# A fused Nystrom attention and mixture-of-experts kernel: halved first loads, landmark trees on VectorE, a W2 half placed later, one ending tile loaded as it lies, and last copies split over two engines

## The chip, the cores and the metric

The kernel runs on one core of a Trainium2 chip. The metric is the device time of one execution in microseconds (us). A run of the profiler gives one execution with every instruction's start and duration; other executions are only timed. PE is TensorE (PEld its weight loads), DVE is VectorE, ACT is ScalarE, POOL is GpSimd and SP is SyncE; a "q" behind a name (SPq, DVEq) means the sequencer of that engine, which waits, branches and issues transfers.

## The reference

The inputs are q, k and v, each 8 batches x 8 heads x 576 positions x 64 (float32), two gate matrices 512x8, and for 8 experts W1 (512x1024) and W2 (1024x512). Cut to what matters:

```python
q_lm = q.reshape(B, H, 32, 18, D).mean(axis=3)        # landmarks: means of 18 rows
k_lm = k.reshape(B, H, 32, 18, D).mean(axis=3)
A, Bm, C = sm(q, k_lm), sm(q_lm, k_lm), sm(q_lm, k)   # softmax of scaled products
Z = Bm.T / (norm1(Bm) * norminf(Bm) + 1e-6)
for _ in range(6):
    Z = 2 * Z - Z @ Bm @ Z
x = (A @ Z @ C @ v)                                   # then laid out as 4608 tokens x 512
e_idx = argmax(x @ w_gate)                            # one expert for each token
out[tok] = softmax(x @ w_gate)[e_idx] * sigmoid((x @ w_output_gate)[e_idx]) * (relu(x @ w1[e]) @ w2[e])
```

## The kernel before, in words

The attention works on 16 groups of one batch and four heads. A group's q and k lie in the upper part of the big expert weight tile `W` (three experts' worth of it, called `tail`, holds attention data until it is free for weights). `load` (L211) issues q, k and v of a group on SP; q and k have two pairs of places, so a load waits until the group two before it has been turned. The first two groups are loaded at the very start, in the order q, k, v, q, k, v. A load of `zeros` into the sorted token buffer `x_sorted` (L163) stands ahead of them in the source, and after the first q and k in SP's order.

`landmark_sums` (L224) adds the 18 rows of each landmark as a tree of five adds on POOL; for group 0 alone DVE makes the sum with one reduction (L948). `landmarks` (L236) scales a sum on ACT and writes it twice side by side. `transposes` (L243) turns a q or k on PE into two PSUM tiles of four blocks and one of two, of which the last block is the landmark; ACT copies each PSUM tile out (L257), and there are two such PSUM tiles in turn (`ps_t`). Then come the score products (L265, L280), the softmaxes, the iteration for Z (L359 to L379, small matmuls with a DVE step between), and the products that give a token's 512 values and its gate logits (L422). `routing` picks the expert of each token on DVE and POOL scatters token rows to `x_sorted` by expert (L530).

The expert part works on tiles of 128 tokens of one expert. Tiles come in stages: 8 and 10 tiles of the fullest two experts, then 8 "free" tiles, all while the attention still runs, and an ending whose number of tiles depends on the data. An ending is one arm of a switch (L967): each engine reads the number of the arm from memory, and jumps to its own code for it. In the profiled run the ending has 12 tiles. For a tile of the first stages `fetch` (L670) loads x as it lies and `turn_x` (L694) turns it with four PE transposes and a DVE copy; an ending tile's x is instead loaded by a transposing transfer (L680). `up` makes h (L720, or L709 in the first two stages), `turn_h` (L725) turns it with eight PE transposes and one DVE copy (L730), `down` (L732) multiplies by W2 in eight matmuls (L737), which can be issued as two halves of four, scales the result on DVE (L743), and POOL scatters the rows to the output (L745). Weights are loaded and cast by POOL's transfers, four pieces an expert (L142 for W1, L145 for W2).

The order of the work is written out by hand. Each kind of work is a generator, and the string `ORDER` (L20) lists which generator makes its next step: L loading, G landmark sums, M landmark scaling, T transposes, C and A the two softmaxes, N the iteration, O outputs, R routing, E weight loads, X expert tiles. A generator that needs an event not yet recorded skips its turn. What comes out is one fixed order of instructions on each engine; each engine works through its own in order and waits at semaphores.

Of the kernel before, what the change touches and what calls it, by code (L numbers as in the profile page):

```python
# [8 lines left out]
F32 = mybir.dt.float32  # L9
# [10 lines left out]
ORDER = (  # L20
    "TTTGTTLTMCTGCTTACGCMCATTCTLMATCCTLAAAAGTCALCMTTCTCNGANLMCNATCGTLALCAACTGMCLTTANTLAMNCCTLGCANCNNLTCAN"
    "AANMGTCCTNNLTATAOLGAMCCNLGATOAACCTMAGNOCANTLTACTMNTANCLMNONNCACNLACNGOTTCGTMCANOALONTTATLOCCNOATNCGA"
    "AMNOCTRRCTCNARLRMNRTTTRLARCLNTNGCMNRRLGRRCRARAAACTCNCLTRTNLRNTAGOTLMATNRTEENRCRCONRCRNAGCNONTAMAACCG"
    "AEOTXTATNONLXCAALNCMGATTACCOTCAEAEXXOMXCOOLXTNMATXGAOLLRTRTNXERGLAXCXXMTXCNTRGCACRMTECCTAATNRARXMNCC"
    "XNXXNARRLTCENTAXCEXNXLTACTXLGTXARAALNLRGRETXXCNXMTNGCNAAXXONRXETXCNXNXAOLXANAOTNRAXNACOMNCGXTONCEXML"
    "TNALCRTXAGOCCXLXOTXXAMCXCAXGRETOCAOXXRCOTNNTTTXXERNXERCMNXXRRXXANREETXEXCNXRXARCRNXRRAXEMXEXREAETXXT"
    "CTXNXTRNRCTXRNXXXCLXAXEXCCEXXXXCRNCOXCEAAOAXXACXXXXXNEAXXAXXEXNOEXXEONXXNXXEOANRXXXXRXXNXXXRENXNXANE"
    "XXXXAXNXXXNAXXOXOOXOXXXOXRRRRRXRXXXXRXXRXXXXRRXXXRRRXXXXXXXXXRRXXXXXXRXXXXXXXRRXXXXXXXXXXXX"
)
# [3 lines left out]
def kernel(  # L33
# [11 lines left out]
    nc = tc.nc  # L45
# [177 lines left out]

    def landmark_sums(k, nm):  # L224
        G = groups[k]
        t = G[nm]
        s = sa.tile([128, hg, D], F32, tag="lms", bufs=1, name="lms")
        s1 = sa.tile([128, 1, D], F32, tag="lm1", bufs=2, name="lm1")
        nc.gpsimd.tensor_tensor(s, t[:, :hg, :], t[:, hg:, :], op=OP.add)  # L229
        nc.gpsimd.tensor_tensor(s[:, 0:4, :], s[:, 0:4, :], s[:, 4:8, :], op=OP.add)  # L230
        nc.gpsimd.tensor_tensor(s[:, 0:2, :], s[:, 0:2, :], s[:, 2:4, :], op=OP.add)
        nc.gpsimd.tensor_tensor(s[:, 0:1, :], s[:, 0:1, :], s[:, 1:2, :], op=OP.add)
        nc.gpsimd.tensor_tensor(s1, s[:, 0:1, :], s[:, 8:9, :], op=OP.add)
        G["s" + nm] = s1
# [8 lines left out]
    def transposes(k):  # L243

        G = groups[k]
        for nm in ("q", "k"):
            tv = G[nm].rearrange("p (gp par) d -> p gp (par d)", par=2)
            lm = G["l" + nm].rearrange("p a d -> p (a d)")
            at = turned_places[(2 * k + (nm == "k")) % 3]
            tT = tail[:, at:at + TW].rearrange("p (c x) -> p c x", x=128)  # L250
            G[nm + "T"] = tT
            for c0 in range(0, hg + 1, 4):
                n = min(4, hg + 1 - c0)
                p = ps_t.tile([128, 4, 128], F32, tag="tp", name="tp")
                for i in range(n):
                    nc.tensor.transpose(p[:, i, :], in_=tv[:, c0 + i] if c0 + i < hg else lm, identity=I128)  # L256
                nc.scalar.copy(tT[:, c0:c0 + n, :], p[:, :n, :])  # L257
                yield
# [191 lines left out]
    def routing(pair):  # L450
# [216 lines left out]
    last = len(SLOTS)  # L667
    xs_bf = xs.bitcast(BF16)

    def fetch(t):  # L670
# [53 lines left out]

    def turn_h(t):  # L725
        pt = ps_t.tile([128, FCH, 128], BF16, tag="tp", name="pt")
        for fc in range(FCH):
            nc.tensor.transpose(pt[:, fc, :], in_=t["h"][:, fc], identity=Ibf)  # L728
        t["hT"] = mp.tile([128, FCH, 128], BF16, tag="h", bufs=3, name="hT")
        nc.vector.tensor_copy(t["hT"], pt)  # L730

    def down(t, part=None):  # L732
        if part != 1:
# [6 lines left out]
        if part == 0:  # L740
            return
        y = mp.tile([128, HD], F32, tag="y", bufs=4, name="y")
        nc.vector.tensor_scalar(out=y, in0=t["py"], scalar1=t["coef"],  # L743
                                scalar2=None, op0=OP.mult)
        i = nc.gpsimd.indirect_dma_start(  # L745
            out=out, out_offset=bass.IndirectOffsetOnAxis(ap=t["id"], axis=0),
# [15 lines left out]
    def summing():  # L762
        for k in range(1, NGRP):
            for nm in "qk":
                yield from need("loaded " + nm, k)
                yield from need("marked " + nm, k - 1)
                landmark_sums(k, nm)
# [12 lines left out]
    def turning():  # L780
        for k in range(NGRP):
            for i, _ in enumerate(transposes(k)):
                if i % 3 == 2:
                    mark("turned " + "qk"[i // 3], k)
                yield
                nxt = 6 * k + i + 1
                if nxt < 6 * NGRP and nxt % 3 == 0:
                    to, half = nxt // 6, nxt % 6 // 3
                    yield from need("marked " + "qk"[half], to)
                    if to + half >= 2:  # L790
# [83 lines left out]
    def working():  # L874
        for stage, n in enumerate(SLOTS):
# [12 lines left out]
            for j, t in enumerate(tiles):  # L888
# [9 lines left out]
                if stage >= len(RANKS):  # L898
                    turn_h(t)
                    yield  # L900
# [45 lines left out]
    for nm in "qk":  # L946
        s1 = sa.tile([128, 1, D], F32, tag="lm1", bufs=2, name="lm1")
        nc.vector.tensor_reduce(s1[:, 0, :], groups[0][nm].rearrange("p g d -> p d g"), axis=AX.X, op=OP.add)  # L948
        groups[0]["s" + nm] = s1
        landmarks(0, nm)  # L950
        mark("marked " + nm, 0)
    for c in ORDER:
# [14 lines left out]
    for arm in tc.Switch(tables["which"], len(ENDINGS), hint="ending"):  # L967
# [40 lines left out]
```

## Time and profile before

| | |
|---|---|
| median of 3 runs | 377.08 us (375.72 to 377.74) |
| the profiled execution's own time | 376.81 us |
| its span, first to last instruction | 375.2 us |
| mean granted TensorE clock | 0.985 |
| PE busy | 323.5 us (86%) |
| DVE, ACT, POOL busy | 221.2, 175.0, 215.5 us |
| moved by the transfers | 66.76 MB, mean 178 GB/s |
| attention and first stages | 0 to about 282 us |
| free tiles alone | about 282 to 318 us |
| ending, 12 tiles | 318.4 us to the end |

A row of the timeline gives start, duration, engine, line, operation, result and inputs, shapes and count, and in brackets how long the engine was idle before it and what ended that. Rows of several like instructions are merged. A row of the waits gives the sum, the number and the longest. A row of the stretches gives, for each engine, busy time and instructions, then the granted PE clock, the share of the 16 transfer engines that was busy and the GB/s. The profiled execution is close to the median of the timed ones, so its stretches can be read as those of an ordinary run.

### The profile page before, as it was taken

The numbers are of one execution on the slowest core, as the hardware profiler recorded it, in microseconds if no ns is written. First come the engines' busy times: TensorE is split into PE (matmuls) and PEld (weight loads), VectorE is DVE, ScalarE is ACT, GpSimd is POOL, SyncE is SP. The second block draws the span as 40 slices with busy tenths as digits, with TensorE's granted clock in tenths as the row PEclk, the third lists the DMA queues.
The fourth block names the chain that finished last, engine by engine and source line by source line (L and its number), as shares of the span: only waits on it lengthen the run. The fifth ranks groups of instructions, "written<-read, shape, count | busy, mean of one in ns | idle before, by whom it ended". The sixth has DMA issues, their size and how long they took to land. (4 is left out here: it accounts for less than half of the span.)

```text
span 375.2 us, 11946 instructions
## 1 busy us (share of the span) xinstructions
PE 323.5 (86%) x4532; PEld 208.1 (55%) x4532; DVE 221.2 (59%) x584; ACT 175.0 (47%) x413; POOL 215.5 (57%) x319
## 2 busy tenths in 40 slices
PE   2888879888888877999998899999979997899992
PEld 1555456565655645676666477666645553455551
DVE  6277677477977384777658672665635674223322
ACT  2676475766737553554555354543234331232320
POOL 3788855644887487278888465784420585122322
PEclk9999899999989998999999999999999999999999
DMA  8866555245637997895587799999992357354221
GB/s 254 268 192 207 176 190 168 71 145 190 184 145 139 293 261 156 216 236 202 116 243 190 146 243 255 228 229 247 228 259 89 117 180 172 64 91 121 73 86 50
DMA packets 46743, 66.76 MB, mean 178 GB/s; under 512 B 16208, under 2 KB 35024, under 8 KB 46672
## 3 DMA queue, kind: packets, MB, share of 16 engines
q0 software_dynamic: 17568, 31.24, 37.4%
q1 hardware_dynamic: 29104, 34.63, 31.9%
q8 instruction: 39, 0.64, 0.7%
q14 instruction: 32, 0.26, 0.3%
HBM read 65.35 MB, written 16.23 MB: 217 GB/s over the span
## 5 line engine op out<-in xcount | busy, mean ns | idle before, releaser
L745 POOL DMA_INDIRECT out_dram<-y,ic x38 | 39.1, 1030 | 88.1 <-DVE y L743 69.9
L737 PE MATMUL py<-W,hT 128*128 (+1 forms) x304 | 73.9, 382 | 6.9 <-DMA W<-in_moe_w_dram 4.0
L743 DVE TENSOR_SCALAR y<-py,ic 128x512 f32<-128x512 f32 x38 | 28.4, 749 | 60.2 <-PE py L737 59.9
L257 ACT COPY W<-tp 128x512 f32<-128x512 f32 (+1 forms) x96 | 47.9, 515 | 31.9 <-PE tp L256 31.6
L256 PE MATMUL tp<-ident,W 128*128 128x128 f32 x288 | 51.2, 298 | 13.3 <-ACT W L257 7.8
L229 POOL TENSOR_TENSOR lms<-W 128x576 f32<-128x576 f32 x30 | 43.0, 1435 | 31.6 <-DMA W<-in_q_dram 30.6
L737 PEld LDWEIGHTS <-hT 128*128 128x128 bf16 x304 | 29.1, 99 | 39.1 <-issue 6.6
L723 ACT ACTIVATE h<-ph 128x512 bf16<-128x512 f32 x40 | 23.9, 597 | 56.0 <-PE ph L720 51.2
L256 PEld LDWEIGHTS tp<-ident,W 128*128 128x128 f32 x288 | 34.5, 148 | 24.5 <-ACT W L257 12.3
L530 POOL DMA_INDIRECT x_sorted<-row,r_slot x36 | 36.7, 1020 | 13.5 <-POOL row L528 8.8
L709 PE MATMUL ph<-xT,W 128*128 128x128 bf16 x576 | 37.7, 219 | 1.5 <-DMA W<-in_moe_w_dram 0.7
L422 PE MATMUL po<-vbd,AT 64*128 64x160 f32 (+1 forms) x320 | 32.8, 324 | 4.4 <-DVE L L428 3.4
L709 PEld LDWEIGHTS <-W 128*128 128x128 bf16 x576 | 33.2, 98 | 4.8 <-issue 2.6
L428 DVE TENSOR_REDUCE L<-po 128x16 f32<-128x128 f32 (+1 forms) x40 | 11.6, 290 | 40.2 <-ACT row L426 40.2
L712 ACT ACTIVATE hT<-ph 128x512 bf16<-128x512 f32 x36 | 21.4, 597 | 27.8 <-PE ph L709 27.6
L426 ACT CAST row<-po 128x512 bf16<-128x512 f32 (+1 forms) x40 | 23.4, 585 | 21.1 <-PE po L422 17.6
L265 PE MATMUL S<-W 64*32 64x288 f32 x512 | 26.1, 466 | 5.7 <-ACT BC L290 4.1
L359 PE MATMUL pw<-WV 32*32 32x96 f32 (+1 forms) x768 | 25.6, 249 | 5.6 <-DVE WV L379 3.4
L422 PEld LDWEIGHTS po<-vbd,AT 64*128 64x128 f32 (+1 forms) x320 | 22.5, 178 | 11.8 <-DVE L L428 5.7
L230 POOL TENSOR_TENSOR lms<-lms 128x256 f32<-128x256 f32 x30 | 24.9, 830 | 2.4
L359 PEld LDWEIGHTS pw<-WV 32*32 32x32 f32 x768 | 15.5, 107 | 16.0 <-DVE WV L379 7.4
L720 PE MATMUL ph<-W,x 128*128 x96 | 22.7, 379 | 1.7 <-DMA out_dram<-y,ic 1.3
(166 smaller groups left out, 530.0 us busy)
## 6 DMA issues: line engine op xcount, KB each, us to landing
W<-in_moe_w_dram POOLq DMA_DIRECT2D x32, 512.0 KB, 11.2
W<-in_q_dram SPq DMA_DIRECT2D x16, 576.0 KB, 6.6
W<-in_k_dram SPq DMA_DIRECT2D x16, 576.0 KB, 6.7
W<-in_v_dram SPq DMA_DIRECT2D x16, 576.0 KB, 5.2
x<-x_sorted SPq DMA_DIRECT2D x26, 128.0 KB, 6.4
x_sorted<-zeros SPq DMA_DIRECT2D x9, 136.0 KB, 1.9
ic<-x_sorted SPq DMA_DIRECT2D x38, 1.0 KB, 5.5
out_dram<-y,ic POOLq DMA_INDIRECT x38, 2.9
```

The lines of the kernel that those rows point to most:

```text
L229: nc.gpsimd.tensor_tensor(s, t[:, :hg, :], t[:, hg:, :], op=OP.add)
L230: nc.gpsimd.tensor_tensor(s[:, 0:4, :], s[:, 0:4, :], s[:, 4:8, :], op=OP.add)
L256: nc.tensor.transpose(p[:, i, :], in_=tv[:, c0 + i] if c0 + i < hg else lm, identity=I128)
L257: nc.scalar.copy(tT[:, c0:c0 + n, :], p[:, :n, :])
L265: nc.tensor.matmul(p[hs, par, :hg * 32], lhsT=lhs[pr, hg, hs], rhs=cols(rhs[pr, :hg, hs]))
L359: nc.tensor.matmul(p[hs, gi, lo:32 + D], lhsT=cur[hs, gi, :32], rhs=cur[hs, gi, lo:])
L422: nc.tensor.matmul(po[ps, hp, gi * 2 * VC:(gi + 1) * 2 * VC], lhsT=ATs[gi][hs, 128 * c:128 * c + n], rhs=vbd[hs, gi].rearrange("p a b -> p ...
L530: i = nc.gpsimd.indirect_dma_start(out=xs, out_offset=bass.IndirectOffsetOnAxis(ap=slot[:, c:c + 1], axis=0), in_=rows[c], in_offset=None)
L709: nc.tensor.matmul(ph[:, 128 * i:128 * i + 128], lhsT=columns(t, dc * F + (half * FCH // 2 + i) * 128, 128), rhs=t["xT"][:, dc, :], start= ...
L737: nc.tensor.matmul(t["py"], lhsT=t["hT"][:, fc, :], rhs=columns(t, DCH * F + fc * HD, HD), start=(fc == 0), stop=(fc == FCH - 1))
L743: nc.vector.tensor_scalar(out=y, in0=t["py"], scalar1=t["coef"], scalar2=None, op0=OP.mult)
L745: i = nc.gpsimd.indirect_dma_start(out=out, out_offset=bass.IndirectOffsetOnAxis(ap=t["id"], axis=0), in_=y, in_offset=None, bounds_check= ...
```

## The change

Five things change.

1. Group 0's q and k are each loaded by two transfers of half the columns, one issued by SP and one by ACT. In SP's order the first v then comes ahead of the zeros.
2. Group 0's landmark sums are made by the same tree of five adds as the other groups', on DVE instead of POOL. The scaling of k's landmark, which stood ahead of the first three PSUM copies on ACT, is now the first step of the generator M, and follows them (a letter M is put into `ORDER`). In `transposes` the landmark is looked up only when its block comes.
3. Two X steps move later in `ORDER`: the second half of the first tile's W2 product and the turn of a following x. On PE, four L737 matmuls and four L697 transposes now stand behind four L256 transposes, ten L359 and L364 matmuls, two more L256 and three L298 transposes. On DVE the y scaling and the xT copy move behind the start of an iteration and a routing step. On POOL the output scatter of that tile moves behind one tree of landmark sums.
4. The first tile of every ending (`LAID = 1`) is loaded as it lies, and turned by `turn_x` inside the arm: four PE transposes and a DVE copy ahead of its first L720.
5. The last free tile's and the last ending tile's hT copies, and the last ending tile's y scaling, are split: DVE makes the first half, ACT the second.

A temporary of the routing also shares its buffer with an earlier one.

```diff
 ORDER = (
-    "TTTGTTLTMCTGC...
+    "TTTMGTTLTMCTGC...
...
-    "...OLLRTRTNXERGLAXCXXMTXCNTRGCACRMTECC...
+    "...OLLRTRTNXERGLAXCXMTCNTRGCXXACRMTECC...
...
-            nc.sync.dma_start(out=t, in_=src.rearrange("h (m g) d -> (h m) g d", g=g))
+            lies = src.rearrange("h (m g) d -> (h m) g d", g=g)
+            if k == 0:
+                nc.sync.dma_start(out=t[:, :hg], in_=lies[:, :hg])
+                nc.scalar.dma_start(out=t[:, hg:], in_=lies[:, hg:])
+            else:
+                nc.sync.dma_start(out=t, in_=lies)
...
-    def landmark_sums(k, nm):
+    def landmark_sums(k, nm, eng):
...
-        nc.gpsimd.tensor_tensor(s, t[:, :hg, :], t[:, hg:, :], op=OP.add)
+        eng.tensor_tensor(s, t[:, :hg, :], t[:, hg:, :], op=OP.add)
...
-        zz = rt.tile([128, CPP, E], F32, tag="r_zz", name="r_zz")
+        zz = rt.tile([128, CPP, E], F32, tag="r_w8", name="r_zz")
...
+    LAID = 1
...
-        if s < last:
+        if s < last or i < LAID:
             ld = nc.sync.dma_start(out=x, in_=xs_bf[bass.ds(row, 128), :HD])
             t["x"] = x
...
-    def turn_h(t):
+    def turn_h(t, split=False):
...
+        if split:
+            nc.vector.tensor_copy(t["hT"][:, :FCH // 2], pt[:, :FCH // 2])
+            nc.scalar.copy(t["hT"][:, FCH // 2:], pt[:, FCH // 2:])
+            return
         nc.vector.tensor_copy(t["hT"], pt)
...
-    def down(t, part=None):
+    def down(t, part=None, split=False):
...
+        n = HD // 2 if split else HD
-        nc.vector.tensor_scalar(out=y, in0=t["py"], scalar1=t["coef"],
+        nc.vector.tensor_scalar(out=y[:, :n], in0=t["py"][:, :n], scalar1=t["coef"],
                                 scalar2=None, op0=OP.mult)
+        if split:
+            nc.scalar.activation(out=y[:, n:], in_=t["py"][:, n:], func=COPY, scale=t["coef"])
...
     def marking():
+        landmarks(0, "k")
+        mark("marked k", 0)
+        yield
...
-                    turn_h(t)
+                    turn_h(t, split=stage == last - 1 and j + 1 == n)
...
     for nm in "qk":
-        s1 = sa.tile([128, 1, D], F32, tag="lm1", bufs=2, name="lm1")
-        nc.vector.tensor_reduce(s1[:, 0, :], groups[0][nm].rearrange("p g d -> p d g"), axis=AX.X, op=OP.add)
-        groups[0]["s" + nm] = s1
-        landmarks(0, nm)
-        mark("marked " + nm, 0)
+        landmark_sums(0, nm, nc.vector)
+    landmarks(0, "q")
+    mark("marked q", 0)
...
             if j == 0:
+                turn_x(t)
                 both(t)
-            turn_h(t)
+            turn_h(t, split=j + 1 == len(run))
...
-            down(t)
+            down(t, split=j + 1 == len(run))
```

More of the change, by code (lines that the diff above doesn't have):

```diff
@@ L20 @@
 ORDER = (
[L21 to L28, printed above, removed]
+    "TTTMGTTLTMCTGCTTACGCMCATTCTLMATCCTLAAAAGTCALCMTTCTCNGANLMCNATCGTLALCAACTGMCLTTANTLAMNCCTLGCANCNNLTCA"
+    "NAANMGTCCTNNLTATAOLGAMCCNLGATOAACCTMAGNOCANTLTACTMNTANCLMNONNCACNLACNGOTTCGTMCANOALONTTATLOCCNOATNCG"
+    "AAMNOCTRRCTCNARLRMNRTTTRLARCLNTNGCMNRRLGRRCRARAAACTCNCLTRTNLRNTAGOTLMATNRTEENRCRCONRCRNAGCNONTAMAACC"
+    "GAEOTXTATNONLXCAALNCMGATTACCOTCAEAEXXOMXCOOLXTNMATXGAOLLRTRTNXERGLAXCXMTCNTRGCXXACRMTECCTAATNRARXMNC"
+    "CXNXXNARRLTCENTAXCEXNXLTACTXLGTXARAALNLRGRETXXCNXMTNGCNAAXXONRXETXCNXNXAOLXANAOTNRAXNACOMNCGXTONCEXM"
+    "LTNALCRTXAGOCCXLXOTXXAMCXCAXGRETOCAOXXRCOTNNTTTXXERNXERCMNXXRRXXANREETXEXCNXRXARCRNXRRAXEMXEXREAETXX"
+    "TCTXNXTRNRCTXRNXXXCLXAXEXCCEXXXXCRNCOXCEAAOAXXACXXXXXNEAXXAXXEXNOEXXEONXXNXXEOANRXXXXRXXNXXXRENXNXAN"
+    "EXXXXAXNXXXNAXXOXOOXOXXXOXRRRRRXRXXXXRXXRXXXXRRXXXRRRXXXXXXXXXRRXXXXXXRXXXXXXXRRXXXXXXXXXXXX"
 )
@@ L228, in landmark_sums @@
         s1 = sa.tile([128, 1, D], F32, tag="lm1", bufs=2, name="lm1")
[L229 to L233, printed above, removed]
+        eng.tensor_tensor(s, t[:, :hg, :], t[:, hg:, :], op=OP.add)
+        eng.tensor_tensor(s[:, 0:4, :], s[:, 0:4, :], s[:, 4:8, :], op=OP.add)
+        eng.tensor_tensor(s[:, 0:2, :], s[:, 0:2, :], s[:, 2:4, :], op=OP.add)
+        eng.tensor_tensor(s[:, 0:1, :], s[:, 0:1, :], s[:, 1:2, :], op=OP.add)
+        eng.tensor_tensor(s1, s[:, 0:1, :], s[:, 8:9, :], op=OP.add)
         G["s" + nm] = s1
@@ L253, in transposes @@
                 n = min(4, hg + 1 - c0)
+                if c0 + n > hg:
+                    lm = G["l" + nm].rearrange("p a d -> p (a d)")
                 p = ps_t.tile([128, 4, 128], F32, tag="tp", name="tp")
@@ L766, in summing @@
                 yield from need("marked " + nm, k - 1)
-                landmark_sums(k, nm)
+                landmark_sums(k, nm, nc.gpsimd)
                 mark("summed " + nm, k)
@@ L786, in turning @@
                 nxt = 6 * k + i + 1
+                to, half = nxt // 6, nxt % 6 // 3
+                if nxt < 6 * NGRP and nxt % 3 == 2:
+                    yield from need("marked " + "qk"[half], to)
                 if nxt < 6 * NGRP and nxt % 3 == 0:
-                    to, half = nxt // 6, nxt % 6 // 3
-                    yield from need("marked " + "qk"[half], to)
+                    yield from need("loaded " + "qk"[half], to)
                     if to + half >= 2:
```

1 line of the change is left out of this document (removed).

## The prediction

> **What bounds the kernel now.** I read the page's busy times first, then the waits of PE, then the timelines of the three places that the change touches.
>
> ```profile
> PE 323.5 (86%) x4532; PEld 208.1 (55%) x4532; DVE 221.2 (59%) x584; ACT 175.0 (47%) x413; POOL 215.5 (57%) x319
> ```
>
> ```profile
> PE tp L256 <- ACT W L257: 7.8, 11, 2.9
> PE tp L256 <- DMA W<-in_q_dram: 4.8, 1, 4.8
> ...
> PE py L737 <- DMA W<-in_moe_w_dram: 4.0, 1, 4.0
> ...
> PE ph L709 <- DMA W<-in_moe_w_dram: 0.7, 1, 0.7
> ```
>
> PE is busy for 86% of the span and works through one fixed order, so it sets the end: time that PE gains at a place is kept unless something else is late behind it. Its large waits are few: 4.8 us for the first q, one of 2.9 us for an ACT copy, one of 4.0 us for a W2 piece. The sum below counts, for each place, how much earlier or later PE reaches the work behind it.
>
> **The start (parts 1 and 2).**
>
> ```profile
> 4.71 4.11 DVE L948 TENSOR_REDUCE lm<-W 128x64 f32<-128x1152 f32 x2 [1.65 <-DMA W<-in_q_dram]
> 23.99 0.76 DVE L333 TENSOR_TENSOR At<-At,a_su 128x576 f32<-128x576 f32 x1
> 29.86 0.23 DVE L350 TENSOR_TENSOR BC<-BC,mB 128x64 f32<-128x64 f32 x1
> ...
> 8.86 0.31 ACT L239 ACTIVATE lm<-lm 128x128 f32<-128x128 f32 x1 [1.68 <-DVE lm L948]
> 9.07 1.05 ACT L257 COPY W<-tp 128x512 f32<-128x512 f32 x2
> 14.19 0.31 ACT L239 ACTIVATE lm<-lm 128x128 f32<-128x128 f32 x1 [1.13 <-POOL lm L233]
> ...
> 9.69 0.47 PE L256 MATMUL tp<-ident,W 128*128 128x128 f32 x1 [2.93 <-ACT W L257]
> 15.47 0.27 PE L256 MATMUL tp<-ident,lm 128*128 128x128 f32 x1
> ...
> 10.62 1.41 POOL L229 TENSOR_TENSOR lms<-W 128x576 f32<-128x576 f32 x1 [6.33 <-DMA W<-in_q_dram]
> ```
>
> ```profile
> 3.00:4.00 1.00, 0.00 (x0) 0.00 (x0) 0.06 (x1) 0.00 (x0) 0.88 (x8) 1.00 1.00 406
> 9.00:10.00 1.00, 0.31 (x2) 0.29 (x2) 0.00 (x0) 1.00 (x3) 0.00 (x0) 1.00 1.00 401
> ```
>
> PE has eight blocks turned by 6.8, but the copies that free their PSUM wait behind k's landmark (8.86), which waits for the second of two reductions of 2.05 us. After the change only q's landmark stands ahead. Its tree, by the 576-wide row (0.76) and the 64-wide one (0.23), is 0.76 + about 0.43 + 0.29 + 0.23 + 0.23 = 1.94 us (the two middle ones interpolated by width), so q's sum is there at 6.65 and the copies start near 6.9 instead of 9.07: 2.2 us.
>
> PE cannot keep that. Group 1's q landmark is written on ACT at 14.19 to 14.50, behind a POOL tree that begins when q of group 1 lands (10.62). PE would want it at 15.47 - 2.2 = 13.3 and gets it at about 14.55. **Gain 0.9 us.** I let that landing stay: the transfer engines are already full from 3 to 10 us, and halving a transfer adds no bytes. The two extra issues on ACT and the swap of v and zeros on SP I cost at nothing: ACT's first need is at 6.7, and the same bytes stand ahead of group 1's q. That the halves bring the first q in no sooner costs nothing for the same reason: even 0.5 us later, PE would still be ahead of that landmark. Queued behind the wait at 14.55 are the score products of group 0 and group 1's k, and through them SP's later loads, which move with PE. Bounds of the gain: 0 (PE cools in the wait that is left, below) and 2.2 (the landing moves too).
>
> **The W2 half (part 3).**
>
> ```profile
> 137.87 1.04 PE L737 MATMUL py<-W,hT 128*128 128x512 bf16 x4
> 142.94 1.87 PE L737 MATMUL py<-W,hT 128*128 128x512 bf16 x4 [4.03 <-DMA W<-in_moe_w_dram]
> 144.60 1.06 PE L256 MATMUL tp<-ident,W 128*128 128x128 f32 x4
> 145.46 0.56 PE L697 MATMUL pt<-ident_bf,x 128*128 128x128 bf16 x4
> ...
> 147.55 0.72 PE L265 MATMUL S<-W 64*32 64x288 f32 x16
> ...
> 140.45 0.76 DVE L284 TENSOR_REDUCE nm<-S 128x1 f32<-128x576 f32 x1
> 146.18 0.75 ACT L288 ACTIVATE eC<-S,nm 128x576 f32<-128x576 f32 x1
> ```
>
> ```profile
> 40.00:44.00 4.00, 2.58 (x56) 1.81 (x47) 2.39 (x8) 1.76 (x5) 3.61 (x6) 0.93 0.67 248
> 44.00:48.00 4.00, 4.00 (x89) 2.25 (x87) 3.21 (x6) 2.01 (x6) 3.61 (x6) 0.65 0.00 1
> ...
> 143.00:144.00 1.00, 1.00 (x3) 0.34 (x3) 0.00 (x0) 0.00 (x0) 0.80 (x3) 0.50 1.22 195
> ```
>
> The work that now fills the wait takes 147.55 - 144.60 = 2.95 us, less 0.49 for L697, which moves along with the half: 2.46 of 4.03 us. Its last part needs eC: nm is ready at 141.2, eC 0.75 later at about 142.0, the three transposes end near 142.5, still ahead of the weights at 142.9. So the half starts when it did, relative to the weights, and what followed it is already done: 2.46 us. The weights themselves come as much earlier as POOL issues them, and POOL works behind loads that wait for PE, so the 0.9 us of the start stays on top. Besides, four matmuls took 1.87 us here against 1.04 before the wait: the granted clock fell to 0.50. If the clock stays up, another 0.83 us: 3.3 us. The longest wait left is some 1.5 us (for eC), less than half of the old one. I take the warm end, **gain 3.3 us**, and keep 2.5 as the lower bound; above 3.3 there is nothing, since the half cannot start before its weights.
>
> [...]
>
> Queued behind the half on PE are the L697 turn and L265, and on DVE y and xT now stand behind an iteration's start and a routing step, some ten short instructions. These have their inputs before the weights land, so DVE is free when the half ends; the readers of y and xT, the scatter and the next up, come after. POOL's scatter behind one tree takes the place of a wait of POOL. Cost nothing; were that cover gone, one tree, by POOL's first row 1.41 and its four narrower adds some 3.2 us, on POOL alone.
>
> **The switch (parts 4 and 5).**
>
> ```profile
> L1003 ACTq COMPARE_BRANCH  x1: 58/58/58, 313.5 to 313.5; - x1
> L1003 PEldq COMPARE_BRANCH  x1: 470/470/470, 317.7 to 317.7; - x1
> L1003 DVEq COMPARE_BRANCH  x1: 83/83/83, 318.7 to 318.7; - x1
> L1003 SPq COMPARE_BRANCH  x1: 63/63/63, 323.4 to 323.4; - x1
> ```
>
> ```profile
> L967 PEldq BRANCH_PREFETCH_HINT  x1: 50/50/50, 318.3 to 318.3; - x1
> L967 ACTq BRANCH_PREFETCH_HINT  x1: 36/36/36, 319.2 to 319.2; - x1
> L967 DVEq BRANCH_PREFETCH_HINT  x1: 45/45/45, 323.4 to 323.4; - x1
> L967 SPq BRANCH_PREFETCH_HINT  x1: 50/50/50, 326.1 to 326.1; - x1
> ```
>
> ```profile
> 319.77 1.89 PE L720 MATMUL ph<-W,x 128*128 x8 [1.34 <-DMA out_dram<-y,ic]
> 367.28 1.95 PE L737 MATMUL py<-W,hT 128*128 x8 [1.08 <-DVE hT L730]
> ...
> 323.56 0.69 DVE L730 COPY hT<-pt 128x1024 bf16<-128x1024 bf16 x1 [4.34 <-PE pt L728]
> ```
>
> ```profile
> L743 DVE TENSOR_SCALAR y<-py,ic 128x512 f32<-128x512 f32 x38 | 28.4, 749 | 60.2 <-PE py L737 59.9
> L699 DVE COPY xT<-pt 128x512 bf16<-128x512 bf16 x26 | 10.6, 415 | 1.3 <-PE pt L697 1.3
> ```
>
> The first fence has each engine's jump to the arm, the second the first instruction of the arm. PE needs 0.6 us, but ACT 5.7, DVE 4.7, SP 2.7. Before, PE starts the first ending tile at 319.77, and DVE is not needed until hT (323.56). After, PE needs DVE for xT before its first L720, everything of the ending is queued behind that on PE, and DVE can jump only when it has issued the last free tile's y. That jump comes 0.27 earlier (half an hT copy is 0.41 by L699, against 0.68), at 318.45. If DVE again needs 4.7 us, it reaches its first copy 0.2 later, and with 0.41 and 0.15 to PE's start L720 comes at 323.9: 4.1 us late. By SP's 2.7 it is 2.1 late, by ACT's 5.7 it is 5.1. DVE's own row is the nearest, and SP's the next: SP jumped when the first transposing loads were through, and since the first x is now a plain load, DVE may find the transfers freer than before. I take the middle of the two, 3.7: **loss 3.1 us**. The turn's four PE transposes lie in the same wait, and so does PE's own read of the tile's weight offset. ACT now jumps later too, after its half of hT near 316, but is needed only when the first four L720s end, near 324; by its 5.7 us it is there.
>
> [...]
>
> The last tile: hT starts PE 0.27 earlier (the wait of 1.08 in front of L737), and y in two halves takes 0.75 / 2 plus some fixed time, about 0.45 on each engine, 0.3 less. **Gain 0.55**; bounds 0.2 and 0.65.
>
> **The sum.** -0.9 - 3.3 + 3.1 - 0.55 = -1.65 us. From the profiled execution (span 375.2, own time 376.81) that is 375.2; it lies 0.27 under the median of the runs shown, so on their scale 375.4, and I give 375.5. A measurement here can tell 0.5%, 1.9 us, from no change: faster means under 375.2.
>
> **Rivals.**
>
> *A, the sum above*, its own range 374.4 (the switch at 2.1) to 377.2 (the switch at 4.1, the W2 gain at 2.5): chance 0.44.
>
> *B, DVE is there in time.* If the jump costs DVE what it costs PE, tile 0 loses only its turn and copy, which lie beside PE's own 1.34 us of idle time: about 0.3. Then -0.9 - 3.3 + 0.3 - 0.55 = -4.45, 372.6. For it: PE's 0.6 us. Against: three engines at the same switch, DVE itself among them. Chance 0.20.
>
> *C, slower.* The advance is lost in the stretch where the transfers are full:
>
> ```profile
> 216.00:281.00 65.00, 61.30 (x913) 42.94 (x912) 35.77 (x106) 27.52 (x61) 36.41 (x47) 1.00 1.15 241
> ```
>
> There the transfer engines are over-full (1.15). If PE runs into weights that do not come earlier, the 4.2 us of the first two gains go, and the rest is +3.1 - 0.55 = +2.55: 379.6. It decides from 3.5 us lost. Against: the view of PE's waits names one long weight load, the one at 143, and PE idles only 3.7 of these 65 us. Chance 0.14.
>
> *D, the clock.* PE's new wait at 13 us and what is left at 141 still halve the clock, as at 44: the start gives nothing, W2 2.5, the sum is -2.5 + 3.1 - 0.55 = +0.05, 377.1. For it: the row at 44, where no single wait was long. Against: PE has 2.5 us of work in the W2 wait that was empty. Chance 0.22.
>
> **How the numbers follow.** B and a little under half of A (375.2 lies just under its middle) are faster: 0.20 + 0.20 = 0.40. The rest of A and most of D are no change: 0.24 + 0.18 = 0.42. C and the edge of D are slower: 0.14 + 0.04 = 0.18. The likeliest is A. The range goes from B (372.6) to D with the switch at ACT's 5.7 (-2.5 + 5.1 - 0.55 = +2.05, 379.1) and leaves out C.
>
> **What would show it.** PE's first copy-released transpose near 7.5 and the group 1 landmark near 14.55; L265 behind the W2 half 3 us nearer to the first half than 9.7; in the arm, DVE's first instruction well behind its jump and PE idle 3 to 5 us before the first L720. Wrong if DVE's jump takes under 1 us, if PE meets a new wait for weights or q between 150 and 310, or if half-clock stretches come in other places.

## The result, and the profile after

The changed kernel took 382.6 us in the median of 6 runs (380.64 to 383.77), the kernel before beside it 377.41 us (375.72 to 381.6, 6 runs). The ratio is 1.0137, with a 95% interval of 1.009 to 1.0184: 5 us slower. A ratio, here and below, leaves out the executions that are more than 1.5% above the fastest of their kernel, while medians are of all executions. 375.5 was forecast, with a range to 379.1, so both the sign and the range were wrong. The profiled execution of the changed kernel took 382.37 us (span 380.7). In the changed code the lines of the prediction have moved: L720 is L727, L737 is L748, L697 and L699 are L704 and L706, L256 and L257 are L262 and L263, L730 is L741 (split: L738 on DVE, L739 on ACT), L743 is L755 (split: with L758), L967 is L984 and L1003 is L1021.

From the profile's page after, the granted clock in 40 slices, and from the waits of PE (sum, number, longest):

```profile
PEclk9999987999998998999999999999999998599999
```

```profile
PE ph L727 <- DMA x_sorted<-row,r_slot: 2.6, 1, 2.6
PE pt L704 <- issue: 2.4, 1, 2.4
...
PE py L748 <- DMA W<-in_moe_w_dram: 0.7, 1, 0.7
```

PE's 4.0 us for the W2 piece have become 0.7. In their place stand two waits of 2.4 and 2.6 us in the ending, and slice 35 of the clock, right behind them, is at 0.5. The timeline of the changed kernel shows the place:

```profile
314.42 0.41 DVE L738 COPY hT<-pt 128x512 bf16<-128x512 bf16 x1
314.87 0.58 ACT L739 COPY hT<-pt 128x512 bf16<-128x512 bf16 x1 [2.25 <-DVE hT L738]
314.98 1.94 PE L748 MATMUL py<-W,hT 128*128 x8 [0.82 <-DVE hT L738]
...
319.30 0.38 PE L704 MATMUL pt<-ident_bf,x 128*128 128x128 bf16 x4 [2.38 <-issue]
321.70 0.42 DVE L706 COPY xT<-pt 128x512 bf16<-128x512 bf16 x1 [3.99 <-issue]
322.26 2.29 PE L727 MATMUL ph<-W,xT 128*128 x5 [2.58 <-DMA x_sorted<-row,r_slot]
...
327.41 3.57 PE L727 MATMUL ph<-W,x 128*128 x8 [0.28 <-PE pt L735]
330.78 2.28 PE L748 MATMUL py<-W,hT 128*128 x8
```

The jumps and the first instructions of the arm (duration in ns, start in us), and two stretches behind them (length, PE busy and instructions, clock, share of the transfer engines, GB/s):

```profile
L1021 PEldq COMPARE_BRANCH  x1: 2730/2730/2730, 316.3 to 316.3; - x1
L1021 DVEq COMPARE_BRANCH  x1: 83/83/83, 317.2 to 317.2; - x1
```

```profile
L984 PEldq BRANCH_PREFETCH_HINT  x1: 50/50/50, 319.1 to 319.1; - x1
L984 DVEq BRANCH_PREFETCH_HINT  x1: 45/45/45, 321.5 to 321.5; - x1
```

```profile
321.90:325.30 3.40, 2.82 (x7) 0.50 0.22 46
325.30:328.70 3.40, 2.86 (x14) 0.50 0.22 39
```

DVE needed 4.3 us from its jump to the arm, near the 4.7 of the prediction's row of DVE, and then made the copy that PE waited for; the wait that the profile books on a transfer ends with that copy (321.70 + 0.42, PE at 322.26). The last of the last free tile's eight py matmuls starts at 316.54, so the first ending ph comes 5.72 us behind it; before it was 1.72 (318.06 to 319.77). Below, "py to ph" is this distance. The granted clock is halved for 10.2 us, and the first ending tile's py (330.78) comes 8.52 us behind its ph, against 5.08 before. Ahead of the switch the changed kernel had been 1.5 us early; it ended 5.5 us late.

### The profile page after: what moved, and what is told of

It reads as the page before. It is cut to its first block, busy times and chain, and to the rows that moved or that the text cites. A ratio compares the mean times of both kernels' runs of the same rounds, so it can differ in the third digit from the quotient of the medians.

```text
span 380.7 us, 11944 instructions
## 1 busy us (share of the span) xinstructions
PE 327.5 (86%) x4507; PEld 210.7 (55%) x4536; DVE 219.5 (58%) x593; ACT 176.2 (46%) x416; POOL 214.6 (56%) x319
## 4 chain that ended last, share of the span: by engine, by line
PE 40%; DMA 23%; POOL 14%; issue 10%; DVE 6%; ACT 5%; POOLq 1%; SPq 0%; ACTq 0%
DMA out_dram<-y,ic 13%; PE py L748 9%; DMA W<-in_q_dram 7%; PE ph L716 6%; PE tp L262 4%; PE pw L365 4%; PE po L428 4%; POOL lms L234 4%; PE S L271 3%; POOL x_sorted L536 3%; PE ph L727 3%; DMA W<-in_moe_w_dram 2%; POOL lms L235 2%; POOL out_dram L759 2%; PE pv L314 2%
## 5 line engine op out<-in xcount | busy, mean ns | idle before, releaser
L748 PE MATMUL py<-W,hT 128*128 (+1 forms) x285 | 71.7, 384 | 4.1 <-DVE hT L738 1.6
L755 DVE TENSOR_SCALAR y<-py,ic 128x512 f32<-128x512 f32 (+1 forms) x38 | 28.2, 742 | 60.9 <-PE py L748 59.6
L262 PE MATMUL tp<-ident,W 128*128 128x128 f32 x288 | 51.0, 297 | 14.0 <-ACT W L263 8.6
L263 ACT COPY W<-tp 128x512 f32<-128x512 f32 (+1 forms) x96 | 48.0, 516 | 26.1 <-PE tp L262 25.7
L730 ACT ACTIVATE h<-ph 128x512 bf16<-128x512 f32 x40 | 23.9, 597 | 60.2 <-PE ph L727 55.1
L748 PEld LDWEIGHTS <-hT 128*128 128x128 bf16 x304 | 29.2, 99 | 35.4 <-issue 4.1
L262 PEld LDWEIGHTS tp<-ident,W 128*128 128x128 f32 x288 | 34.3, 148 | 24.9 <-ACT W L263 12.7
L719 ACT ACTIVATE hT<-ph 128x512 bf16<-128x512 f32 x36 | 21.4, 596 | 27.7 <-PE ph L716 27.5
L432 ACT CAST row<-po 128x512 bf16<-128x512 f32 (+1 forms) x40 | 23.4, 584 | 23.0 <-PE po L428 21.0
L365 PEld LDWEIGHTS pw<-WV 32*32 32x32 f32 x768 | 15.2, 106 | 15.3 <-DVE WV L385 7.1
L727 PE MATMUL ph<-W,x 128*128 x84 | 22.1, 403 | 0.4 <-PE pt L735 0.3
```

Source lines behind the costliest of these rows:

```text
L365: nc.tensor.matmul(p[hs, gi, lo:32 + D], lhsT=cur[hs, gi, :32], rhs=cur[hs, gi, lo:])
L727: nc.tensor.matmul(ph, lhsT=t["xT"][:, dc, :], rhs=columns(t, dc * F + half * (F // 2), F // 2), start=(dc == 0), stop=(dc == DCH - 1))
L748: nc.tensor.matmul(t["py"], lhsT=t["hT"][:, fc, :], rhs=columns(t, DCH * F + fc * HD, HD), start=(fc == 0), stop=(fc == FCH - 1))
```

## The experiments

A ratio below is to the kernel before on the same chip. Chips differ: the kernel before takes about 379 us on two of those used here, and 396 to 400 on two others.

**One part at a time (first chip, before 400.09 us).** Theory 1 is that the laid tile costs and the other parts gain.

Without part 4:

```diff
-        if s < last or i < LAID:
+        if s < last:
...
-                turn_x(t)
                 both(t)
```

> The changed kernel without part 4: the first ending tile is loaded by a transposing transfer again and not turned in the arm. Theory 1 (the laid tile is the whole loss: in the trace of after, PE's first L727 of the ending comes 4.0 us later against the work before it than in the trace of before, and the half clock behind it costs some 3.5 us more): about 375 us, 1 to 3 us under before, and PE idle at most 1.5 us at the switch. Rival 1 (the other parts lose too, since after was already 1.4 us late at 132 us): 378 to 380.

The kernel before with part 4 alone (the same lines put in):

> The kernel before with part 4 alone. Theory 1: 4 us of waiting and 3.5 us of half clock, 383 to 386 us, with a stretch of half clock near 320 to 332 us. Rival 2 (the wait alone costs; the half clock in the trace of after was chance): 380.5 to 382, and no half clock behind the switch.

The kernel before with part 3 alone:

```diff
-    "...OLLRTRTNXERGLAXCXXMTXCNTRGCACRMTECC...
+    "...OLLRTRTNXERGLAXCXMTCNTRGCXXACRMTECC...
```

> The kernel before with part 3 alone, the later W2 half. As the two traces read (1.4 us late at 132 us, 1.4 us early at 174 us): 2.5 to 3 us gained, 374.5 to 375 us. Rival (the clock halves elsewhere instead, so that the gain is lost): 376.5 to 377.5.

The kernel before with parts 1 and 2 alone (halved loads, DVE trees, the moved scaling of k's landmark):

> The kernel before with parts 1 and 2 alone. The prediction's term: 0.9 us gained, 376.5 us, PE's group 1 landmark near 14.55 us. New theory (on ACT the scaling of group 1's q landmark stands ahead of the copies of group 1's q, so that PE waits for POOL's tree through ACT whatever comes before): 0 gained, 377 to 378 us, and PE's second score product at 16.1 us as before.

Measured: 0.9972 [0.9901, 1.0042], 0.9963 [0.9881, 1.0046], 0.9969 [0.9884, 1.0054] and 0.9971 [0.9904, 1.0039], medians 397.4 to 398.3. The times decide nothing. The traces tell more: with the laid tile the first ending ph comes 4.51 us behind the last free py, without it 1.78 and 1.66. The third, without a laid tile, had 3.77, because PE's own jump took 2.47 us there:

```profile
L1003 PEldq COMPARE_BRANCH  x1: 2470/2470/2470, 339.2 to 339.2; - x1
```

That made a second theory: PE's own long jump, and not the laid tile, is what costs.

**The laid tile (second chip, before 378.59 us).** Four kernels side by side: the change again; the change without the laid tile (the edit above); the laid tile turned ahead of the jump; and fillers in PE's wait.

```diff
     for t in rest[:HELD]:
         fetch(t)
+    turn_x(rest[0])
     for arm in tc.Switch(tables["which"], len(ENDINGS), hint="ending"):
...
-                turn_x(t)
                 both(t)
```

```diff
                 turn_x(t)
+                fill = ps_t.tile([128, DCH, 128], BF16, tag="tp", name="fill")
+                for n in range(36):
+                    nc.tensor.transpose(fill[:, n % DCH, :], in_=t["x"][:, 128 * (n % DCH):128 * (n % DCH) + 128], identity=Ibf)
                 both(t)
```

> The changed kernel again, beside the next three on one chip. Theory 1 (the laid tile's turn inside the arm makes PE wait for DVE's jump, and the clock halves behind that wait): last free-tile py to first ending ph 4.5 to 5.7 us, first ending ph to its py 6.5 to 8.5 us with a half-clock stretch in it, time 1.0 to 1.6% over the kernel without the laid tile. Theory 2 (PE's own jump is what was long, by where its code lies, whether a tile is laid or not): PE's jump takes 2.5 to 2.8 us here and, where it takes 0.5 elsewhere, that kernel is faster whether its tile is laid or not. Theory 3 (the start and the W2 half lose by half-clock stretches in other places): it stands to before as the kernel without the laid tile does.

> The changed kernel without part 4 (the first ending tile loaded by the transposing transfer again). Theory 1: last free-tile py to first ending ph 1.7, ph to py 5.1, no half clock behind the switch; 0.3 to 0.9% under before (W2 half and split copies stay). Theory 2: as the changed kernel if its PE jump takes 2.5 us, else faster by 2.3. Theory 3: 1% over before, as the changed kernel.

> The laid tile stays, but is turned ahead of the switch: PE's four transposes and DVE's copy stand behind the last free tile's work and ahead of both jumps, so PE needs nothing of DVE behind its jump until hT. Theory 1: last free-tile py to first ending ph 1.9 to 2.6 us (the turn's 0.4 on PE, PE's jump of 0.5; with a jump of 2.8 it is 4.5), ph to py 5.1, time as the kernel without the laid tile within 0.3%. Theory 2: as the changed kernel, 1.0 to 1.6% over the kernel without the laid tile, with a PE jump of 2.5 us or more. Theory 3: as the changed kernel.

> The changed kernel with 36 more PE transposes of the laid tile (their result is not used) between its turn and its first L727. They take about 36 x 0.055 = 2.0 us, by four in 0.22 of the turn, and lie in PE's wait for DVE, so they should not put off the first ph. If the half clock behind the switch comes from that wait: ph to py 5.1 to 6.8 instead of 8.5, and 1.7 to 3.4 us under the changed kernel. If the half clock has nothing to do with the wait (it comes by where the clock's windows fall, or from the stretch before the jump): ph to py stays as in the changed kernel, within 0.5 us, and so does the time.

| kernel | median, 12 runs each | ratio to before | last free py to ending ph | ph to its py | PE's jump to the arm |
|---|---|---|---|---|---|
| the change | 380.61 | 1.0081 [1.0042, 1.012] | 5.97 | 6.77 | 0.52 |
| without the laid tile | 377.45 | 0.9988 [0.9946, 1.0029] | 1.80 | 5.08 | 0.43 |
| turned ahead of the jump | 378.45 | 0.992 [0.987, 0.997] | 1.86 | 5.08 | 0.53 |
| with fillers | 378.19 | 1.0027 [0.999, 1.0065] | 5.12 | 5.08 | 2.54 |

The timeline's PE rows with the turn ahead of the jump, and then with the fillers, which end at 320.5:

```profile
319.48 0.39 PE L704 MATMUL pt<-ident_bf,x 128*128 128x128 bf16 x4
321.12 1.89 PE L727 MATMUL ph<-W,xT 128*128 x8 [1.26 <-DVE xT L706]
```

```profile
318.13 0.38 PE L705 MATMUL pt<-ident_bf,x 128*128 128x128 bf16 x4 [2.14 <-issue]
320.74 1.89 PE L728 MATMUL ph<-W,xT 128*128 x7 [0.21 <-DVE xT L707]
```

The laid tile costs 3.2 us by the medians, 0.9% by the ratios. Theory 2 is refuted for the changed kernel: its jump on PE took 2.73 us in one execution and 0.47 in the next, and the ph came 5.72 and 5.97 us behind. DVE's jump (4.35 and 4.60 us) sets it, PE's hides in it. Where nothing hides it, PE's long jump does cost: in four executions with no turn behind the jump (part 3 alone, and further below parts 1 and 2 alone, the split copies alone and the moved scaling) it left py to ph at 3.7 to 4.7 us. Turning the tile ahead of the jump takes the wait for DVE away while the tile stays laid; its median gives back 2.2 us of the 3.2, its ratio, which counts 6 of its 12 executions, all. The fillers leave py to ph at 5.12 us, but the eight ph matmuls behind it come at full speed, and 2.4 us are gained by the medians: the half clock behind the switch comes from PE's idle time there. It is one execution with fillers, but the others bear it out: in all eight without fillers in which py to ph was 3.7 us or more, ph to py was 6.4 to 8.5 us, whatever caused the wait, and in the eleven others 5.1 to 5.2.

**Each part alone, once more (first chip, before 397.25 us).** Part 3, parts 1 and 2, and part 4 as above, and part 5 alone (the split copies of the diff).

> The kernel before with part 3 alone (the W2 half and the turn of a following x later), on one chip with the three other parts, each alone. Theory 1 (the prediction's term): 2.5 to 3.3 us under before, ratio 0.991 to 0.993. Rival (the wait for the W2 piece is mostly replaced by the wait for eC behind the same late softmax, 1.4 to 2.2 us as the runs without the laid tile show it): 1.0 to 2.6 us, ratio 0.993 to 0.997. If the weights are in time in the kernel before as well: 0, ratio 1.000.

> The kernel before with parts 1 and 2 alone (halves of the first q and k, trees on DVE). The prediction's term: 0.9 us under before, ratio 0.9976. Theory of ACT's order (the landmark of group 1's q stands ahead of that group's copies on ACT, so that PE has its first wait less and a later one more): 0, ratio 0.999 to 1.002; where the longer wait at 13 to 15 us lets the clock halve, up to 1.7 us slower, ratio up to 1.0045.

> The kernel before with part 5 alone (split copies of the last free and the last ending tile). The prediction's term: 0.55 us under before. Theory that the halves run one after the other (ACT's half waits for DVE's, as in the trace of the changed kernel): hT still starts PE 0.26 earlier twice, but the last scatter starts 0.23 later behind the last py (1.68 instead of 1.45 us), together 0.3 us or less: ratio 0.999 to 1.000, and in the trace 1.68 us from the last L737 to the scatter.

> The kernel before with part 4 alone (first ending tile loaded as it lies, turned in the arm). The prediction's term: 3.1 us over before, ratio 1.008. With half clock behind the switch on top: up to 6 us, ratio 1.016. In the trace 4.5 to 6 us from the last free-tile py to the first ending ph instead of 1.7. If the switch does not take DVE longer than PE: within 0.3 us of before.

Measured: 1.0153 [1.0099, 1.0207] (7 runs), 1.0232 [1.0173, 1.0291] (6), 1.0009 [0.9963, 1.0055] (13) and 1.0074 [1.0033, 1.0115] (12). The laid tile is at the prediction's 3.1 us (0.0074 of 397 is 2.9), and 4.83 us lie between the last free py and the first ending ph. The split copies show no gain. The first two contradict the earlier 0.9969 and 0.9971 of the very same kernels on the same chip, with intervals that do not meet: with 4 to 7 runs an interval here is too narrow. In none of the traces of part 3 on this chip was a W2 piece late, and in the five on this chip that have the old order at that place PE waited for the piece 0.7 us at most.

**The start and the W2 half once more (third chip, before 378.78 us, 12 runs each),** with two versions of the turn ahead of the jump: one with the scaling of group 1's q landmark moved behind that group's copies on ACT, one with the last y scaled whole.

```diff
-    "TTTMGTTLTMCTGCTTAC...
+    "TTTMGTTLTCTGCTMTAC...
```

```diff
-            down(t, split=j + 1 == len(run))
+            down(t)
```

> The kernel before with part 3 alone, once more, beside part 1 and 2 alone. Theory (the wait for eC takes the place of most of the wait for the weights): where before waits 4 us for that W2 piece, 1.0 to 2.6 us under before, ratio 0.993 to 0.997, with a wait of 1.4 to 2.4 us for eC at about 148 us in the trace. The prediction's term: 2.5 to 3.3 us, 0.991 to 0.993. If its second measurement on the other chip holds everywhere: 1.010 or more.

> The kernel before with parts 1 and 2 alone, once more. Theory of ACT's order: nothing gained, ratio 0.999 to 1.002, up to 1.0045 where the clock halves at 13 to 20 us. The prediction's term: 0.9976. If its second measurement on the other chip holds everywhere: 1.017 or more.

> The laid tile turned ahead of the switch, and the scaling of group 1's q landmark moved behind that group's copies on ACT. If ACT's order is what kept the start from gaining: PE's copy-released wait at about 15.5 us (0.95 to 2.2 us in the runs so far) is gone or under 0.4, the scores of group 0 (the first S behind the landmark's transpose) start by 15.6 instead of 16.1 to 16.4, and the kernel is 0.3 to 1 us faster than with the turn ahead alone. If the landmark itself is what is late: the wait stands in front of its transpose instead, and nothing is gained. Time to before 0.989 to 0.997.

> The laid tile turned ahead of the switch, and the last y scaled whole on DVE (the split of hT stays). If the split y costs what the traces show: the last scatter starts 1.45 us behind the last L748 instead of 1.68, 0.23 us gained, not to be told in the time. Time to before 0.989 to 0.998, as with the turn ahead alone.

Part 3 alone: 375.55 us, 0.9974 [0.9931, 1.0016]. Parts 1 and 2 alone: 381.93 us, 1.0089 [1.0031, 1.0147]. Moved scaling: 376.72, 0.9987 [0.994, 1.0035]. Whole y: 377.35, 1.0004 [0.9954, 1.0055].

The timeline of part 3 alone shows the W2 half:

```profile
138.14 1.04 PE L737 MATMUL py<-W,hT 128*128 128x512 bf16 x4
...
142.38 0.81 PE L298 MATMUL tp<-ident,eC 128*96 128x128 f32 x3 [1.43 <-ACT eC L288]
142.98 1.91 PE L737 MATMUL py<-W,hT 128*128 128x512 bf16 x4
```

The wait of 4.03 us is one of 1.43 for eC, and the weights are there: 2.6 us of PE's waiting are gone. Four matmuls still took 1.91 us, so the clock was not kept in this execution.

The start needs more rows. PE's rows of the kernel before, and of the change without the laid tile (most executions with the halved loads start like this):

```profile
13.12 0.89 PE L265 MATMUL S<-W 64*32 64x288 f32 x16 [0.46 <-ACT W L257]
...
13.97 1.09 PE L256 MATMUL tp<-ident,W 128*128 128x128 f32 x8
...
16.11 0.72 PE L265 MATMUL S<-W 64*32 64x288 f32 x16 [0.37 <-ACT BC L290]
...
21.18 0.88 PE L265 MATMUL S<-W 64*32 64x288 f32 x16
```

```profile
11.28 1.22 PE L271 MATMUL S<-W 64*32 64x288 f32 x16 [0.46 <-ACT W L263]
...
12.50 1.97 PE L262 MATMUL tp<-ident,W 128*128 128x128 f32 x8
15.56 0.48 PE L262 MATMUL tp<-ident,W 128*128 128x128 f32 x1 [1.09 <-ACT W L263]
...
16.37 1.22 PE L271 MATMUL S<-W 64*32 64x288 f32 x16
...
22.77 0.88 PE L271 MATMUL S<-W 64*32 64x288 f32 x16
```

With the halves PE is 1.8 us ahead at the first scores (11.28 against 13.12), and has lost it at the second (16.37 against 16.11). Then it falls behind, since its matmuls take up to twice as long: eight transposes 1.97 us against 1.09, sixteen scores 1.22 against 0.72. The third scores come at 22.77 instead of 21.18. Of eleven executions with the halves nine were like this (third scores at 22.1 to 23.4, the other two at 20.9 and 21.2), of seven without two (22.7 and 23.1, the others 21.2 to 21.4).

What takes the 1.8 us away is seen in the changed kernel's own timeline (POOL, ACT and PE):

```profile
10.96 1.41 POOL L234 TENSOR_TENSOR lms<-W 128x576 f32<-128x576 f32 x1 [6.68 <-DMA W<-in_q_dram]
...
14.53 0.31 ACT L244 ACTIVATE lm<-lm 128x128 f32<-128x128 f32 x1 [3.36 <-POOL lm L238]
14.75 0.57 ACT L263 COPY W<-tp 128x512 f32<-128x512 f32 x1
...
15.37 0.33 PE L262 MATMUL tp<-ident,W 128*128 128x128 f32 x1 [2.19 <-ACT W L263]
```

PE waits for a copy that stands behind group 1's landmark on ACT, so it goes on 0.84 us after the scaling begins. The landmark is later too: POOL's tree begins when group 1's q lands, at 10.6 to 11.9 with the halves and at 10.5 to 10.7 without. The moved scaling puts the copies first. The wait then went to the landmark's own transpose (1.03 us at 15.90), and the second scores came at 16.30. That does not clear ACT's order, since the sum was ready at 14.13 and the scaling, now behind eC and another copy on ACT, came at 15.51:

```profile
13.81 0.32 POOL L238 TENSOR_TENSOR lm<-lms 128x64 f32<-128x64 f32 x1
...
15.51 0.34 ACT L244 ACTIVATE lm<-lm 128x128 f32<-128x128 f32 x1
```

No run has both the copies and the scaling in time.

**PE warmed at the start (fourth chip, before 396.26 us).** Thirteen more PE transposes of the identity ahead of the first q, where PE is idle; with parts 1 and 2 alone, and with part 3 as well.

```diff
+    warm = ps_t.tile([128, 4, 128], F32, tag="tp", name="warm")
+    for n in range(13):
+        nc.tensor.transpose(warm[:, n % 4, :], in_=I128, identity=I128)
     for c in ORDER:
         advance(c)
```

> The kernel before with parts 1 and 2 alone, and 13 more PE transposes of the identity (result not used) ahead of the first q, from about 1.6 to 4.8 us, where PE is idle. Theory of the cold start: the executions with halves lose because PE goes through its first 20 us at half speed (eight transposes in 1.94 to 1.97 us instead of 1.09, scores in 1.22 instead of 0.88), which the fillers end. Then the first q's eight transposes or at the latest those at 12 us take about 1.1 us, the third group of scores starts by 21.2 instead of 22.6 to 23.2, and the kernel is 1.5 to 2.5 us under the same without fillers: ratio to before 0.999 to 1.003 instead of 1.009 and 1.023. If the start loses by its waits or by the landing of group 1's q instead: third scores at 22.5 or later, ratio 1.007 or more.

> The same with part 3 (the later W2 half) added; no laid tile, no split copies. By the cold start: the gain of the W2 half alone (375.6 against 378.8, 3 us) is kept, ratio 0.990 to 0.998, and 1.5 to 2.5 us under the kernel without the laid tile. By the rival (waits or landing): 0.997 to 1.001, as the kernel without the laid tile.

Measured: 1.0056 [1.0002, 1.0109] (12 runs) and 1.0117 [1.0022, 1.0213] (6). The second has few executions and a wide interval, but it lies above what either theory expected of it (0.998 and 1.001 at most). Rows of the first, PE's timeline and stretches:

```profile
8.06 0.33 PE L262 MATMUL tp<-ident,W 128*128 128x128 f32 x1 [1.79 <-ACT W L263]
...
12.46 1.09 PE L262 MATMUL tp<-ident,W 128*128 128x128 f32 x8
15.28 0.33 PE L262 MATMUL tp<-ident,W 128*128 128x128 f32 x1 [1.73 <-ACT W L263]
...
23.36 0.88 PE L271 MATMUL S<-W 64*32 64x288 f32 x16
```

```profile
8.50:12.00 3.50, 2.99 (x26) 0.56 1.03 366
12.00:15.60 3.60, 1.87 (x32) 0.96 1.12 236
15.60:19.00 3.40, 3.03 (x36) 0.52 0.54 216
19.00:22.40 3.40, 3.40 (x57) 0.50 0.24 42
```

PE was fast at 8.06, slow in the stretch from 8.5, fast again at 12.46, and slow again from 15.6 to 22.4, each time behind a wait of 1.7 to 1.8 us for a copy. So the cold start is not the whole cause: behind the wait of 1.73 us in front of group 1's landmark, which is 0.24 us in the kernel before, the granted clock goes from 0.96 to 0.52, and what the fillers gave is lost. Whether this wait also makes the start slow where no filler ran is not shown: no run took the wait away, and in the rows of the change without the laid tile PE is slow (1.22 us at 11.28, 1.97 at 12.50) ahead of that wait already.

## Why the prediction was wrong

In the result's own trace the sum missed by 2.3 us up to 132 us (PE 1.4 us late there instead of 0.9 early), by 0.5 at the W2 half, and by 4.3 at the switch, which is the step that failed most there. Beside the kernel before on the third chip, the start failed most.

**"Gain 0.9 us" at the start.** Parts 1 and 2 cost 3.2 us by the medians of the third chip (381.93 against 378.78), 0.9% by the ratio; the two measurements on the first chip, 0.9971 and 1.0232, lie on both sides. The prediction had PE go on when group 1's landmark is there, at 14.55, and let the landing of that group's q stay. PE waited for the copy behind the landmark instead, and the landing came later: PE's landmark transpose comes at 15.2 to 16.6 with the halves and at 15.47 before, so the gain is 0.3 at best. What was missed besides is the loss: the bounds were 0 and 2.2, and the lower one had in brackets that PE cools in the wait that is left. Slow matmuls in the first 20 us have a price, about 1.6 us at the third scores (22.77 to 21.18), and the prediction counted them as no gain instead of a loss. Rival D had this mechanism and the same price of nothing. Why the slow start is more frequent with the halves stays open.

The result's own trace does not have this loss (third scores at 21.18, as before). It loses 2.9 us between 48 and 62 us: PE's landmark transpose is 1.1 us early at 48.34, and the next one, at 61.83, is 1.8 us late. Both kernels have the same wait there. PE's rows before and after:

```profile
54.46 0.72 PE L265 MATMUL S<-W 64*32 64x288 f32 x16 [1.64 <-ACT BC L290]
```

```profile
53.32 0.72 PE L271 MATMUL S<-W 64*32 64x288 f32 x16 [1.64 <-ACT BC L296]
```

Stretches of 3.41 us around it, in PE's columns alone, before and after. They are cut in steps from the start of a half-clock stretch of the same execution, since the half-clock stretches of these two executions last 3.41, 6.83 or 10.24 us, except at their ends:

```profile
50.23:53.65 3.42, 2.51 (x40) 1.00 1.06 327
53.65:57.06 3.41, 2.30 (x37) 1.00 0.34 135
```

```profile
51.65:55.07 3.42, 1.55 (x24) 1.00 0.59 239
55.07:58.48 3.41, 3.35 (x28) 0.50 0.00 0
```

Before, the wait is shared by two steps and the clock stays up; in the changed kernel it lies in one, and the clock is halved for the next two (0.50 to 61.89). This is a matter of the execution as much as of the kernel: of the eleven executions with the halves four lose 2.9 to 3.2 us at this place, two 1.0 to 1.2 and five next to nothing; of the seven without, two lose 2.9. The prediction named half clock in other places as a sign of being wrong, and put no price on it.

**"Gain 3.3 us" at the W2 half**: 2.8 us in the change's own trace (from 1.4 us late at 132 us to 1.4 early at 174), 2.6 of wait with part 3 alone, 3.2 us by that kernel's median (375.55), 1.0 by its ratio, whose interval reaches from a gain of 2.6 to a loss of 0.6. The filled wait was right. That the clock stays up behind a wait of some 1.5 us was the author's estimate, and the 0.83 for it depends on the execution: behind 1.47 us for eC the change's four matmuls took 1.03 us on the second chip, behind 1.43 us, with part 3 alone, they took 1.91. On the second and third chip the four matmuls took 1.02 to 1.03 us in five profiles with the moved half, and 1.86 and 1.91 with the fillers and with part 3 alone; in the result's own it was 1.74. On the first chip, where that piece was not late, nothing can be gained there.

**"Loss 3.1 us" at the switch** was right in place and cause, DVE's own jump (4.35 and 4.60 us; that it would come nearer to SP's 2.7 with freer transfers was the author's estimate, and no run shows it), but it was sized by the wait alone. In the result's trace the wait cost 4.0 us at the first ph and the half clock behind it 3.4 more, for which the sum had no term. In the traces of the second chip the two are 4.2 (5.97 against 1.80) and 1.7 (6.77 against 5.08), while the time there is 3.2 us (380.61 against 377.45): that this is close to 3.1 is in part luck, and why it is under the 5.9 us of the traces is open. That PE's own jump can take 2.7 us was not foreseen either, and cost nothing here, since DVE's is longer.

**"Gain 0.55" for the split copies**: none that the times show, though the interval of the split copies alone (0.9963 to 1.0055) would hold 0.55 us. The wait ahead of L748 went from 1.08 to 0.82 as worked out, but the halves of y do not run beside each other. In the change's timeline the second waits for the first:

```profile
373.31 1.89 PE L748 MATMUL py<-W,hT 128*128 x8 [0.82 <-DVE hT L738]
375.24 0.48 DVE L755 TENSOR_SCALAR y<-py,ic 128x256 f32<-128x256 f32 x1 [2.07 <-PE py L748]
375.75 0.47 ACT L758 ACTIVATE y<-py,ic 128x256 f32<-128x256 f32 x1 [1.97 <-DVE y L755]
376.50 0.97 POOL L759 DMA_INDIRECT out_dram<-y,ic  x1 [2.41 <-ACT y L758]
```

The scatter starts 3.19 us behind the first L748, with a whole y 3.02 (367.31 to 370.33 in that kernel, as before: 367.28 to 370.30). So the last tile gains 0.26 us ahead of the last py and loses 0.17 behind it. Two writers of one tile were put in order, which the prediction did not look up.

**The rivals.** B is refuted (DVE was not in time in any of five executions). C is refuted as a mechanism: the 1.3 to 1.4 us of advance at 174 us was still there at 310. D was right that the clock can halve again at both places that it named, though not in every execution; it took the two gains back (0.9 and 0.8 us), and had no price for work that becomes slower than before.

The sum by the runs: +3.2 (start) - 3.2 (W2) + 3.2 (switch) + 0 = +3.2 us by medians, between the 2.0 us of the second chip (380.61 against 378.59) and the 5.2 of the first result. By the ratios it is +3.4 - 1.0 + 3.5 = +5.9 us, against 3.1 for the whole change on the second chip, so the parts are known to about 3 us and no better.

No version was shown to beat the kernel before beyond doubt. Part 3 alone has the lowest median (375.55) with an interval that holds 1; the change with the turn ahead of the jump has the best ratio (0.992, from half of its executions), but a median hardly lower than that of the kernel before (378.45 and 378.59), and two close variants of it have 0.9987 and 1.0004.

## What to carry to other kernels

A gain that ends in a wait is not bounded by zero: here the matrix engine came 1.1 us earlier to a wait of 1.64 us that both kernels have, the clock halved behind it in the changed kernel's profile and not in the other's, and 2.9 us were lost there. Price that as a loss, and compare more than one profile of each kernel before a difference is put down to the change. Look at what another engine must do between a jump and the first matmul behind it: the laid tile's turn, which waits there for DVE, cost 3.2 us by the medians, and 2.2 of them came back when it was done ahead of the jump. When work is split over two engines that write one tile, look in the trace or in the waits whether the halves overlap at all: here ACT's half of y began at 375.75, behind the end of DVE's at 375.72.

## What the runs showed of the hardware

From its jump to the first instruction of the arm PE took 0.42 to 0.53 us in 14 of 20 executions and 2.5 to 3.2 in the six others, of one and the same kernel too (part 3 alone: 2.53 on the first chip, 0.51 in its second measurement there), while DVE took 3.0 to 4.8 and ACT 2.7 to 5.7 in all of them.

With the fillers the clock halved behind single waits of 1.79 and 1.73 us: the stretches from 8.5 and 15.6 read 0.56 and 0.52, and PE was busy for 2.99 of their 3.50 and 3.03 of their 3.40 us. It differs between executions: with the halves, and no fillers at the start, the third scores came at 20.9 to 23.4 us.

The granted clock does not show every slow stretch of these traces. A stretch of the change without the laid tile, in PE's columns alone:

```profile
12.50:15.00 2.50, 1.97 (x15) 1.00 1.19 205
```

It reads 1.00 while eight transposes take the 1.97 us quoted above, against 1.09 in the kernel before.
